# Gate and up gradients of a SwiGLU backward pass: four half-token stores per group from SyncE in place of sixteen from ScalarE, silu and its slope in quarters

## The chip, the cores and the metric

The kernel runs on one core of one Trainium2 chip. The metric is the device time of one execution in microseconds (us), as the median of several. A core has a matrix engine (TensorE, PE in the profile; its weight loads are PEld), a vector engine (VectorE, DVE), an activation engine (ScalarE, ACT), a general engine (GpSimd, POOL) and SyncE (SP), which here does nothing but issue transfers. Each engine works off its own instructions strictly in the order in which the compiler laid them down. An instruction that has to wait holds up everything behind it on that engine. This holds for the instruction that starts a transfer too: it sits in the queue of the engine that issues it.

## The reference

The forward function is `x + s * g`. `xn` is the layer norm of `x` (2048 tokens by 576), `s` is a state-space convolution of `xn`, and `g` is silu of a SwiGLU feed-forward network with 4608 hidden units. The kernel returns the output and the gradients of `x` and of all parameters. For the part that the change touches, only this matters:

```python
gate = xn @ w1                       # 2048 x 4608
up   = xn @ w3
h    = silu(gate) * up
out  = h @ w2
# backward, with go the gradient of out (2048 x 576):
gh    = go @ w2.T                    # 2048 x 4608
gup   = gh * silu(gate)              # "gu" in the kernel
ggate = gh * up * silu'(gate)        # "gg" in the kernel
gw2 = h.T @ go;  gw3 = xn.T @ gup;  gw1 = xn.T @ ggate
gxn = ggate @ w1.T + gup @ w3.T + (gradient through the convolution)
```

## The kernel before

The program has a forward half and a backward half. In the forward half, `gate` and `up` are computed and kept in device memory (`G_dram`, `U_dram`), in the layout [group, 128 partitions, 16 token tiles, 256 hidden units]. The backward half is laid out by `backward` (line 1062) and has three strands that share the engines:

- the convolution's backward (`conv_bwd_quarter`, four quarters), then the gradients of its parameters (`param_quarter`, 36 chunks; each loads a transposed `qT` on SyncE and works mainly on VectorE, lines 971 and 974);
- the **groups** of the feed-forward network, 18 of 256 hidden units each. A group is an elementwise half (`phase6_elementwise`) and a half that forms weight gradients (`phase6_weight_grads`), which is laid down one group later;
- `phase6_inputs`, which needs the gate and up gradients of all groups, and so comes last. For each of the 16 token tiles it reads them back, transposed by the transfer itself (`ggc`, `guc`, issued on SyncE), and multiplies them with the transposed weights.

The order on each engine comes from a planner. Calls of `self.at(us)` give each piece a due time, which serves as its priority; the planner simulates the engines and picks, whenever one is free, the ready instruction with the earliest priority. Groups are due every 36 us from 700, quarters of the convolution every 60 us from 700, chunks of the parameters every 16 us from 940, so that the strands interleave.

The elementwise half of one group goes like this. GpSimd loads two raw blocks of `w2` (`w2r6`, line 1131), fills them up (1132), and SyncE transposes them into `w2T` (1133, which runs the helper on line 1115). GpSimd loads `gate` into `gg_n` (1137) and `up` into `h_n` (1138), 1 MB each. ScalarE forms silu into `gu_n` (1139) and silu's derivative over `gg_n` (1140), one instruction each over all 16 token tiles, 4096 elements in each partition. VectorE multiplies with `up` in four slices (1143, 1144). Then come four steps (loop at 1146), each over four token tiles: two of the first half of the tokens and two of the second. In a step, TensorE forms `gh` in two PSUM tiles `ph` (1157, 20 matmuls, three `ph` buffers in all), ScalarE copies both to `gh6` (1160), and VectorE multiplies `gh6` into `gu_n` and `gg_n` (1163). After each of these two products ScalarE issues two stores (1166) of two token tiles each. A group has sixteen stores of 128 KB.

The weight half accumulates over all 16 token tiles into `pgw` tiles in PSUM, of which there are two. Two rounds of two tiles give the `w2` gradient (1183, copied by ScalarE on 1187 into `gw2`), eight rounds give those of `w3` and `w1` (1194, copied on 1197 into `gw13`), and one gives the 64 remaining rows of both (1201 and 1203, copied on 1206). GpSimd issues the store of each copy (1188, 1198, 1207, 1208). The pool of `gw2` and `gw13` has two buffers of each, the pool of `gh6` two.

Of the kernel before, what the change touches and what calls it, by code (L numbers as in the profile page):

```python
# [10 lines left out]
ACT = mybir.ActivationFunctionType  # L11
# [49 lines left out]
class K:  # L61
# [1000 lines left out]
    def backward(self, T0, TG, TQ, TC, TX, gctx, mats):  # L1062
        nc, cfg = self.nc, self.cfg
        D, L, LT, F, FT = cfg.D, cfg.L, cfg.LT, cfg.F, cfg.FT
        self.GG_dram = self.dram.tile([LT, P, F], BF16, name="GG_dram")
        self.GU_dram = self.dram.tile([LT, P, F], BF16, name="GU_dram")
        self.GXN_dram = self.dram.tile([P, LT, D], FP32, name="GXN_dram")
        NG = F // self.FG
        T2 = T0 + TG * NG
        FA = 12  # L1070
        pool = self.tc.tile_pool
        PS = bass.MemoryType.PSUM
        with ExitStack() as out:
            ffn = ExitStack()
            wp = ffn.enter_context(pool(name="e_w", bufs=2))
            inp = ffn.enter_context(pool(name="e_in", bufs=2))
            elp = ffn.enter_context(pool(name="e_el", bufs=2))
            gwp = ffn.enter_context(pool(name="e_gw", bufs=2))
            ps_h = ffn.enter_context(pool(name="e_ps_h", bufs=3, space=PS))
            ps_gw = ffn.enter_context(pool(name="e_ps_gw", bufs=2, space=PS))  # L1080
            ps = out.enter_context(pool(name="b_ps", bufs=3, space=PS, side="right"))
            self.ssm_bwd_conv(T0, TQ, ps)
            mats.close()
            fix = out.enter_context(pool(name="b_fix", bufs=1, side="right"))
            S_all = fix.tile([P, 4, D], FP32, name="S_all")
            wA = out.enter_context(pool(name="x_wA", bufs=1, side="right"))
            self.at(T2 - 150)
            wT = [self.load_wT(wA, 0, FA)]
            T1 = T0 + 4 * TQ
            self.ssm_bwd_params(T1, TC, S_all, ps)  # L1090
            self.at(T1 + TC * D // 16)
            self.phase5_final(out, fix, S_all, ps)
            for gi in range(NG + 1):
                self.at(T0 + TG * gi)
                if gi < NG:
                    tiles = self.phase6_elementwise(gi, wp, inp, elp, ps_h)
                if gi > 0:
                    self.phase6_weight_grads(gi - 1, prev, self.go_o, gwp, ps_gw)
                prev = tiles
            ffn.close()  # L1100
            gctx.close()
            self.phase6_inputs(T2, TX, FA, wT)
# [14 lines left out]
    def phase6_elementwise(self, gi, wp, inp, elp, ps_h):  # L1117
        nc, cfg = self.nc, self.cfg
        D, DT, LT = cfg.D, cfg.DT, cfg.LT
        aps = self.aps  # L1120
        FG = self.FG
        nfl = FG // P
        nfull = D // P
        rem = D - nfull * P
        LH = LT // 2
        assert 2 * rem == P
        w2T = wp.tile([P, nfl, DT, P], BF16, name="w2T")
        for fl in range(nfl):
            fi = gi * nfl + fl
            w2r = wp.tile([P, DT * P], BF16, name="w2r6")  # L1130
            nc.gpsimd.dma_start(out=w2r[:, 0:D], in_=aps["B_w2"][fi * P:(fi + 1) * P, :])
            nc.gpsimd.tensor_copy(out=w2r[:, D:DT * P], in_=w2r[:, nfull * P:D])
            self.nat_transpose(w2T[:, fl], w2r[:])
        gg = inp.tile([P, LT, FG], BF16, name="gg_n")
        hn = inp.tile([P, LT, FG], BF16, name="h_n")
        gu = inp.tile([P, LT, FG], BF16, name="gu_n")
        nc.gpsimd.dma_start(out=gg[:], in_=self.G_dram[gi])
        nc.gpsimd.dma_start(out=hn[:], in_=self.U_dram[gi])
        nc.scalar.activation(out=gu[:], in_=gg[:], func=ACT.Silu)  # L1139
        nc.scalar.activation(out=gg[:], in_=gg[:], func=ACT.Derivative_silu)  # L1140
        for s in range(4):
            sl = slice(s * LT // 4, (s + 1) * LT // 4)
            nc.vector.tensor_tensor(out=gg[:, sl, :], in0=gg[:, sl, :], in1=hn[:, sl, :], op=ALU.mult)
            nc.vector.tensor_tensor(out=hn[:, sl, :], in0=gu[:, sl, :], in1=hn[:, sl, :], op=ALU.mult)
        pair = lambda t_: t_[:].rearrange("p (j t) f -> p j t f", j=2)
        for s in range(LH // 2):
            gh = elp.tile([P, 2, 2, FG], BF16, name="gh6")
            ph = [ps_h.tile([P, 2, FG], FP32, name="ph") for _ in range(2)]
            for k in range(2):
                t = s * 2 + k  # L1150
                for j in range(2):
                    tt = j * LH + t
                    rs = slice(j * rem, (j + 1) * rem)
                    steps = [(self.goT[:, c, tt * P:(tt + 1) * P], w2T[:, :, c, :]) for c in range(nfull)]
                    steps.insert(nfull * (1 - j), (self.goTt[rs, t * P:(t + 1) * P], w2T[rs, :, nfull, :]))
                    for n, (lw, rh) in enumerate(steps):
                        nc.tensor.matmul(ph[j][:, k, :].rearrange("p (a f) -> p a f", f=P), lhsT=lw, rhs=rh, start=(n == 0),  # L1157
                                         stop=(n == nfull))
            for j in range(2):
                nc.scalar.copy(out=gh[:, j], in_=ph[j][:])  # L1160
            sl = slice(s * 2, s * 2 + 2)
            for (dst, t_) in ((self.GU_dram, gu), (self.GG_dram, gg)):
                nc.vector.tensor_tensor(out=pair(t_)[:, :, sl], in0=gh[:], in1=pair(t_)[:, :, sl], op=ALU.mult)
                for j in range(2):
                    ts = slice(j * LH + s * 2, j * LH + s * 2 + 2)
                    nc.scalar.dma_start(out=dst[ts, :, gi * FG:(gi + 1) * FG].rearrange("t p f -> p t f"), in_=t_[:, ts, :])
        return hn, gg, gu

    def phase6_weight_grads(self, gi, tiles, go_o, gwp, ps_gw):
# [196 lines left out]
```

## Time and profile before

| | |
|---|---|
| time, median of 3 | 2269.04 us (2255.82 to 2273.89) |
| profiled execution | 2250.77 us, span of the core 2249.0 us |
| mean granted TensorE clock | 0.93 |
| busy: PE, DVE, ACT, POOL | 82%, 66%, 42%, 20% of the span |
| groups: first `ph` matmul to last `pgw` matmul | 875.7 to 1860.1 us |
| parameter chunks on VectorE (line 971) | 1325.7 to 2095.3 us |
| matmuls of `phase6_inputs` (line 1238) | 1872.9 to 2242 us |
| stores of line 1166 | 288 of 128 KB, issue 0.48 us, landing 3.4 us (medians) |

The profile lists, for each engine, how long it was busy, and for each idle stretch the instruction whose end released it ("releaser"). An instruction that starts a transfer isn't counted as busy time of its engine but occupies its queue all the same: time in which ScalarE is held by its own stores shows up as idle time of the copy behind them, with the transfer as its releaser. "issue" is time in which an engine waited for nothing that the profile shows.

### The profile page before, as it was taken

How to read it: one execution, taken by the hardware profiler on the slowest of the kernel's cores; microseconds unless marked ns; L12 is line 12 of the kernel's file. 1: busy time of each engine (PE TensorE's matmuls, PEld its weight loads, DVE VectorE, ACT ScalarE, POOL GpSimd, SP SyncE). 2: the span in 40 equal slices, each digit the busy share in tenths (PEclk: the TensorE clock that was granted, in tenths of full speed). 3: DMA queues.
4: the chain of work that ended last, by engine and by line, in shares of the span. 5: the costliest groups of instructions: out<-in, count | busy, mean ns of one | idle time of the engine just before them, and what ended most of it. 6: DMA issues, size and time to landing. Idle time of an engine off the chain costs nothing.

```text
span 2249.0 us, 41101 instructions
## 1 busy us (share of the span) xinstructions
PE 1842.5 (82%) x16141; PEld 1268.9 (56%) x16214; DVE 1488.6 (66%) x2842; ACT 950.1 (42%) x1608; POOL 459.0 (20%) x710
## 2 busy tenths in 40 slices
PE   2878888889996997887888857888888883899958
PEld 1533333345544675665767645666666672677736
DVE  7457888879872554887694976756666762186742
ACT  2958888875541114656464613334333330000000
POOL 4024555551122111201121111211111110000000
PEclk9989999999997998999999978999999996999979
DMA  3777777776569886454554579677777759999783
GB/s 76 269 253 261 267 265 264 261 245 240 195 157 244 190 203 160 139 146 118 154 156 143 155 184 198 182 186 150 177 191 176 177 126 199 183 218 221 152 126 77
DMA packets 620339, 420.76 MB, mean 187 GB/s; under 512 B 419504, under 2 KB 559920, under 8 KB 615536
## 3 DMA queue, kind: packets, MB, share of 16 engines
q1 hardware_dynamic: 482464, 240.40, 44.9%
q0 software_dynamic: 29520, 109.15, 15.2%
q10 hardware_dynamic: 108160, 68.57, 11.6%
q8 instruction: 127, 2.08, 0.4%
q14 instruction: 68, 0.56, 0.1%
HBM read 135.37 MB, written 190.37 MB: 145 GB/s over the span
## 4 chain that ended last, share of the span: by engine, by line
PE 26%; DVE 16%; DMA 14%; issue 9%; ACT 7%; SPq 4%; POOL 1%; ACTq 1%; POOLq 0%; DVEq 0%
PE px L1238 9%; SPq L1115 4%; PE pgw L1194 4%; PE ph L1157 3%; DMA w2T<-w2r 2%; PE et_ps L598 2%; DVE cm_t L622 2%; DMA qT<-Q_dram 2%; DMA out_dram<-gw 2%; PE pgw L1183 2%; DMA guc<-GU_dram 2%; ACT gg_n L1140 1%; ACT gu_n L1139 1%; PE pg L739 1%; PE pgw L1201 1%
## 5 line engine op out<-in xcount | busy, mean ns | idle before, releaser
L971 DVE TENSOR_TENSOR pr_q<-et_ps,pz 128x512 f32<-128x512 f32 x288 | 186.5, 684 | 171.6 <-PE et_ps L964 157.9
L1194 PEld LDWEIGHTS <-xn_bf 128*128 128x128 bf16 x2304 | 232.2, 101 | 85.7 <-issue 50.9
L1238 PE MATMUL px<-wTB_w,ggc 128*128 128x288 bf16 x1152 | 245.8, 293 | 35.2 <-DMA ggc<-GG_dram 13.7
L1238 PE MATMUL px<-wTB_w,guc 128*128 128x288 bf16 x1152 | 245.2, 293 | 29.6 <-DMA guc<-GU_dram 18.6
L739 PEld LDWEIGHTS <-xnT 128*128 128x128 bf16 x1152 | 108.7, 100 | 190.9 <-issue 93.5
L739 PE MATMUL pg<-wmB_w,xnT 128*128 128x512 bf16 x531 | 156.4, 399 | 57.9 <-DVE g_t L745 47.1
L974 DVE TENSOR_REDUCE S_all<-pr_q 128x8 f32<-128x512 f32 x288 | 185.3, 680 | 0.2
L1157 PE MATMUL ph<-w2T,goT 128*128 128x256 bf16 x1152 | 171.1, 283 | 12.5 <-DMA w2T<-w2r 6.7
L1183 PE MATMUL pgw<-go_o,h_n 128*128 128x288 bf16 x1152 | 166.0, 301 | 16.4 <-ACT gw L1187 16.0
L1194 PE MATMUL pgw<-gg_n,xn_bf 128*128 128x256 bf16 x1152 | 140.5, 283 | 36.5 <-ACT gw L1197 36.4
L794 PE MATMUL po<-w2g,hc 128*128 128x288 bf16 x1152 | 148.8, 292 | 17.5 <-DMA a<-UH_dram 17.3
L739 PE MATMUL pu<-wmB_w,xnT 128*128 128x512 bf16 x554 | 157.3, 395 | 6.5 <-ACT u_t L748 5.2
L1238 PEld LDWEIGHTS <-guc 128*128 128x128 bf16 x1152 | 114.7, 100 | 71.2 <-DMA guc<-GU_dram 20.3
L1157 PEld LDWEIGHTS <-goT 128*128 128x128 bf16 x1152 | 100.7, 100 | 86.4 <-issue 52.8
L1238 PEld LDWEIGHTS <-ggc 128*128 128x128 bf16 x1152 | 114.9, 100 | 59.3 <-issue 14.2
L1194 PE MATMUL pgw<-gu_n,xn_bf 128*128 128x256 bf16 x1152 | 140.4, 280 | 9.2 <-ACT gw L1187 7.6
L1197 ACT CAST gw<-pgw 128x256 bf16<-128x256 f32 x144 | 52.7, 389 | 224.6 <-DMA out_dram<-gw 89.8
L1255 ACT ACTIVATE t<-gx 128x576 f32<-128x576 f32 x16 | 11.0, 685 | 320.6 <-DVE gx L1241 285.6
L1183 PEld LDWEIGHTS <-h_n 128*128 128x128 bf16 x1152 | 115.7, 103 | 53.0 <-issue 17.7
L794 PEld LDWEIGHTS <-hc 128*128 128x128 bf16 x1152 | 113.6, 100 | 49.4 <-issue 18.2
L1160 ACT CAST gh<-ph 128x512 bf16<-128x512 f32 x144 | 81.1, 601 | 138.0 <-PE ph L1157 34.1
L1241 DVE TENSOR_TENSOR gx<-px,gxs 128x288 f32<-128x288 f32 x32 | 13.4, 452 | 179.4 <-PE px L1238 179.4
(308 smaller groups left out, 3971.6 us busy)
## 6 DMA issues: line engine op xcount, KB each, us to landing
G_dram<-g_t POOLq DMA_DIRECT2D x72, 256.0 KB, 3.5
U_dram<-u_t POOLq DMA_DIRECT2D x72, 256.0 KB, 4.1
H_dram<-h_t SPq DMA_DIRECT2D x72, 256.0 KB, 3.8
Q_dram<-q_k SPq DMA_DIRECT2D x36, 512.0 KB, 3.2
gg_n<-G_dram POOLq DMA_DIRECT2D x18, 1024.0 KB, 5.8
h_n<-U_dram POOLq DMA_DIRECT2D x18, 1024.0 KB, 6.1
GU_dram<-gu_n ACTq DMA_DIRECT2D x144, 128.0 KB, 3.3
GG_dram<-gg_n ACTq DMA_DIRECT2D x144, 128.0 KB, 3.5
```

The costliest lines, as they stand in the source:

```text
L598: nc.tensor.matmul(pv, lhsT=mat[:, kt, sl], rhs=V[:, :, ri, kt, :], start=(i == 0), stop=(i == n - 1))
L739: nc.tensor.matmul(pt[:], lhsT=xnT[:, c, ts], rhs=wm[w][:, c, :], start=(c == 0), stop=False)
L794: nc.tensor.matmul(po_[:, pi_, 0:pw], lhsT=hc[:, fi, :], rhs=w2[fi][:, po:po + pw], start=(fi == 0), stop=(fi == FT - 1))
L971: nc.vector.tensor_tensor(out=pr[:], in0=T[h][:].rearrange("p r d k a -> p (r d) k a"), in1=pz[:, dg, h, s:s + 2].rearrange("p r d a -> p ...
L974: nc.vector.tensor_reduce(out=S_all[:, 2 * s:2 * s + 2, d0:d0 + 4].rearrange("p k d -> p d k"), in_=pr[:].rearrange("p (r d) k a -> p d k ...
L1115: self.nc.sync.dma_start_transpose(out=dst, in_=src)
L1157: nc.tensor.matmul(ph[j][:, k, :].rearrange("p (a f) -> p a f", f=P), lhsT=lw, rhs=rh, start=(n == 0), stop=(n == nfull))
L1160: nc.scalar.copy(out=gh[:, j], in_=ph[j][:])
L1183: nc.tensor.matmul(pgw[pi_][:, 0:pw], lhsT=hn[:, tt, fl * P:(fl + 1) * P], rhs=go_o[:, tt, po:po + pw], start=(tt == 0), stop=(tt == LT - 1))
L1194: nc.tensor.matmul(pw_[:, 0:FG], lhsT=self.xn_bf[:, tt, c * P:(c + 1) * P], rhs=nat[:, tt, :], start=(tt == 0), stop=(tt == LT - 1))
L1197: nc.scalar.copy(out=gw[:], in_=pw_[:, 0:FG])
L1238: nc.tensor.matmul(px[pi_][:, 0:pw], lhsT=act[:, fi, :], rhs=wT[part][ai][:, f, po:po + pw], start=(fi == 0 and ai == 0), stop=(fi == FT - ...
```

## The change

The change has four parts. The stores of `gu_n` and `gg_n` move out of the loop of steps: a group now has four, each of eight token tiles (one half of the tokens) of one tensor, 512 KB, and they are issued by SyncE. Silu runs as four instructions of four token tiles each, and so does its derivative, so that VectorE can begin on a quarter. The pool of `gh6` grows from two buffers to three. The pool of `gw2` and `gw13` grows from two buffers of each to four. The aim is to take the issue of stores out of ScalarE's queue and to loosen the ties between ScalarE, VectorE and the stores.

```diff
@@ backward
-            elp = ffn.enter_context(pool(name="e_el", bufs=2))
-            gwp = ffn.enter_context(pool(name="e_gw", bufs=2))
+            elp = ffn.enter_context(pool(name="e_el", bufs=3))
+            gwp = ffn.enter_context(pool(name="e_gw", bufs=4))
@@ phase6_elementwise
-        nc.scalar.activation(out=gu[:], in_=gg[:], func=ACT.Silu)
-        nc.scalar.activation(out=gg[:], in_=gg[:], func=ACT.Derivative_silu)
-        for s in range(4):
-            sl = slice(s * LT // 4, (s + 1) * LT // 4)
+        quarters = [slice(s * LT // 4, (s + 1) * LT // 4) for s in range(4)]
+        for sl in quarters:
+            nc.scalar.activation(out=gu[:, sl, :], in_=gg[:, sl, :], func=ACT.Silu)
+        for sl in quarters:
+            nc.scalar.activation(out=gg[:, sl, :], in_=gg[:, sl, :], func=ACT.Derivative_silu)
+        for sl in quarters:
             nc.vector.tensor_tensor(out=gg[:, sl, :], in0=gg[:, sl, :], in1=hn[:, sl, :], op=ALU.mult)
             nc.vector.tensor_tensor(out=hn[:, sl, :], in0=gu[:, sl, :], in1=hn[:, sl, :], op=ALU.mult)
...
-            for (dst, t_) in ((self.GU_dram, gu), (self.GG_dram, gg)):
+            for t_ in (gu, gg):
                 nc.vector.tensor_tensor(out=pair(t_)[:, :, sl], in0=gh[:], in1=pair(t_)[:, :, sl], op=ALU.mult)
-                for j in range(2):
-                    ts = slice(j * LH + s * 2, j * LH + s * 2 + 2)
-                    nc.scalar.dma_start(out=dst[ts, :, gi * FG:(gi + 1) * FG].rearrange("t p f -> p t f"), in_=t_[:, ts, :])
+        for (dst, t_) in ((self.GU_dram, gu), (self.GG_dram, gg)):
+            for j in range(2):
+                ts = slice(j * LH, (j + 1) * LH)
+                nc.sync.dma_start(out=dst[ts, :, gi * FG:(gi + 1) * FG].rearrange("t p f -> p t f"), in_=t_[:, ts, :])
```

## The prediction

> **What bounds the kernel now.** I read the page first, for the engines' shares, then the busy time by stretches, then who waited for whom in the stretch of the groups (850 to 1850 us), TensorE first and ScalarE second, then the timeline of ScalarE over one group. The engines and three stretches (the columns are length, then busy time of PE, PEld, DVE, ACT and POOL with the number of instructions, then granted clock, DMA share and GB/s):
>
> ```profile
> PE 1842.5 (82%) x16141; PEld 1268.9 (56%) x16214; DVE 1488.6 (66%) x2842; ACT 950.1 (42%) x1608; POOL 459.0 (20%) x710
> ...
> 1100.00:1200.00 100.00, 87.35 (x893) 69.91 (x893) 80.09 (x166) 62.17 (x144) 16.62 (x26) 0.98 0.50 145
> ...
> 1500.00:1600.00 100.00, 81.97 (x691) 61.21 (x689) 67.06 (x112) 36.85 (x50) 18.70 (x37) 0.92 0.73 174
> 1600.00:1700.00 100.00, 84.33 (x730) 64.83 (x729) 61.80 (x103) 38.27 (x54) 20.29 (x41) 0.95 0.71 169
> ```
>
> TensorE is the busiest engine everywhere, at 81% (773.8 of 950 us from 850 to 1800), and ScalarE is far from full. So the groups are bound by TensorE plus the gaps in it, about 176 us up to 1800. What ends the gaps:
>
> ```profile
> PE ph L1157 <- ACT gh L1160: 44.3, 27, 7.3
> PE pgw L1194 <- ACT gw L1197: 37.4, 21, 10.7
> PE et_ps L964 <- DMA qT<-Q_dram: 17.5, 4, 10.2
> PE pgw L1183 <- ACT gw L1187: 16.0, 7, 7.5
> ...
> PE pgw L1194 <- ACT gw L1187: 7.6, 14, 2.9
> ```
>
> The columns are microseconds in total, times, longest. The four lines with ACT make 105.3 us, and all are PSUM copies of the groups: TensorE has a full PSUM tile and ScalarE hasn't emptied it. Why does an engine that is 42% busy come late? Its own waits answer:
>
> ```profile
> ACT gw L1197 <- DMA out_dram<-gw: 84.9, 34, 5.5
> ...
> ACT gw L1197 <- DMA GG_dram<-gg_n: 32.7, 4, 14.2
> ACT gh L1160 <- DMA GU_dram<-gu_n: 32.7, 7, 6.4
> ACT gw L1197 <- DMA GU_dram<-gu_n: 31.0, 6, 7.1
> ...
> ACT gh L1160 <- DMA GG_dram<-gg_n: 12.9, 2, 7.4
> ```
>
> Two holders stand out: ScalarE is held by the issue of its own stores (32.7 + 32.7 + 31.0 + 12.9 = 109.3 us), and a copy can't start because both `gw13` buffers are still being stored (84.9 us). The timeline of ScalarE in one group shows the first:
>
> ```profile
> 1491.23 1.04 ACTq L1166 DMA_DIRECT2D GU_dram<-gu_n  x2
> 1492.37 1.45 ACTq L1166 DMA_DIRECT2D GG_dram<-gg_n  x2
> 1493.92 1.68 ACTq L1166 DMA_DIRECT2D GU_dram<-gu_n  x2
> 1495.69 1.53 ACTq L1166 DMA_DIRECT2D GG_dram<-gg_n  x2
> 1497.34 0.37 ACT L1197 CAST gw<-pgw 128x256 bf16<-128x256 f32 x1 [5.86 <-DMA GU_dram<-gu_n]
> ```
>
> From 1491.2 to 1497.2 ScalarE does nothing but start eight stores, while a finished `pgw` tile waits.
>
> [...] 288 issues by 0.48 us are 138 us of ScalarE's queue. [...]
>
> **The change part by part.**
>
> *Stores off ScalarE.* Per step ScalarE has two `gh` copies (2 x 0.586 us, the median of line 1160) and four issues (4 x 0.48), 3.1 us; TensorE needs 2.4 us for the step's 20 matmuls (in the timeline at 1609 us, 10 come every 1.2 us). ScalarE is slower by 0.7 us a step, 2.8 us a group, 50 us over 18 groups. The measured `ph` wait is 44.3 us, so this account fits. Without the issues the step costs ScalarE 1.2 us, and a copy no longer stands behind a store that waits for VectorE. I take all 44.3 us as removed. The third `gh6` buffer belongs to this: VectorE may then lag three steps of a group's four.
>
> *Four `gw` buffers.* A round of line 1194 takes 3.65 us on TensorE; copy, issue and landing take 0.37 + 0.54 + 2.2 = 3.1 us, so two buffers do until GpSimd is held. It is held, in its turn, for the `w2T` transposes (119.9 us over 25 waits on line 1131). Example: the transposes are issued at 1591.0 and GpSimd is through its second `w2r` load at 1598.7, 7.7 us, a little over the two rounds (7.3 us) that two buffers cover. Four cover 14.6 us. With the stores gone as well, I take the 37.4 + 1.1 us of lines 1194 and 1201 behind `gw` 1197 as removed. Sum so far: 82.8 us.
>
> *Silu in quarters.* Six more activations per group by the fixed cost: [...] 0.16 us from the copies in the trace (0.373 us for 256 elements, 0.586 for 512: 0.83 ns each, 0.16 left). That is 1.0 to 1.1 us a group. Table loads stay at two a group, as copies between them needed none before. The first product on VectorE waits for 1.28 + 4 x 1.03 + 1.28 + 1.03 = 7.7 us after the load instead of 9.8. Silu has the earlier priority over the `gw` copies of the group before, so I don't expect copies to slip in between the quarters. Then the `gw` 1187 waits (16.0 + 7.6 us) stay, and ten or so of these get 1 us longer: +10 us. The earlier start of VectorE I cost at nothing: line 1163 is behind the `gh` copies and other strands' work (29.8 us of waits on `gh`).
>
> *Stores on SyncE.* This is the new wait. The nearest row is `gK_dram<-gk_st` (line 922): 576 KB in runs of 512 bytes like these stores, 0.65 us to issue, 5.0 us to land (4.7 to 8.2), two at a time. Four stores are 2.6 us of SyncE's queue, hidden by its idleness. But they wait for the last product of line 1163, a few us after the last `ph` matmul, and behind them stand the `w2T` transposes for the group after next, then `qT` and `gz` of the parameter chunks. The 2 MB need 9 us (at 1.13 MB per 5.0 us) to 15 us (per 8.2 us). Lower bound: the planner puts `w2T` first, as it is ready once `ph` ends, and nothing is lost. Upper bound: transposes land 10 to 15 us late each group. Then GpSimd's hold grows from 7.7 to about 18 us, 3 us beyond what four buffers cover, and `qT` (two buffers, one chunk per 21 us: 26 chunks from 1310 to 1865) is late too: 6.5 us a group or 117 us in all, as an estimate. I take 1.2 us a group, 22 us, since only the `w2T` part bites when stores go first, and they go first in perhaps half of the groups.
>
> *Sum.* -82.8 + 10 + 22 = -51 us. A tenth of it I give to waits that come up next (`qT`, VectorE at 80% in the convolution): -45 us. The last 389 us of the span, from the end of the groups, have none of these stores but the transposes of `ggc`, `guc` and weights on SyncE; nothing changes there. 2269 - 45 = **2224 us**.
>
> **The rivals.**
>
> *All of it goes* (0.15): the quarters let copies through and SyncE costs nothing, so all 106 us of copy waits vanish: 2163 us. For it: ScalarE then has about half of its queue free. Against it: the priorities just named.
>
> *Other waits take the place* (0.17): VectorE is 80% busy in the convolution's stretch and waits 145 us for `et_ps` in the parameters, so that in-order TensorE may find the next gap at once; about 10 us remain, 2259 us. Against it: most copy waits are within the group strand itself, where TensorE has some 41 us of work per group (its lines' busy time by 18) in a 48 us cycle.
>
> *SyncE becomes the holder* (0.18): the upper bound above, 2269 - 83 + 117 = 2303 us, **slower**. For it: `qT` already ends 17.5 us of TensorE's waits, and SyncE blocks in order. Against it: `w2T` is prefetched by two groups, and one chunk has 21 us where VectorE needs 11.
>
> **How the numbers follow.** The forecast (0.50) is 2224 us. Faster by over 1% means under 2246: forecast and first rival, 0.65; within 1%: 0.17; slower: 0.18. The range is 2160, where all copy waits are gone, to 2290, inside the SyncE case, which leaves out about 0.1 above and somewhat less below.
>
> **What would show it.** Right: `ph` behind `gh` and `pgw` 1194 behind `gw` 1197 fall from 82 us to under 25; ScalarE's waits on `out_dram<-gw` fall from 84.9 us to under 30; the group cycle from 1400 to 1850 shrinks from 48 to about 45 us; the four stores issue in about 0.65 us each; `gw` 1187 waits stay near 24 us; the tail after the groups stays near 389 us. Wrong: waits of TensorE on `qT`, `w2T` or GpSimd's on `w2T` that grow by more than 40 us; a SyncE queue held by the stores' issue for several us; table loads above 36; a lower granted clock that eats the closed gaps; or a longer tail, if the parameter chunks fall behind the groups.

## The result and the profile after

The changed kernel takes 2172.6 us (median of 4, 2159.7 to 2178.6) against 2270.2 us before: a ratio of 0.9574 with a 95% interval of 0.9516 to 0.9632, so 98 us less where the prediction said 45 us. 1% of the time before is 22.7 us; the shares below are turned into microseconds with it. The profiled executions, from which the lines come, are 91 us apart (2250.77 and 2159.66 us).

First the engines' line of the changed kernel's page, which answers to the one of before:

```profile
PE 1820.9 (84%) x16214; PEld 1260.4 (58%) x16214; DVE 1487.1 (69%) x2842; ACT 960.5 (45%) x1716; POOL 464.8 (22%) x710
```

The work is the same and the span is shorter. Where the time went is read from three stretches of each kernel: from the first `ph` matmul to the first parameter product on VectorE (the convolution), from there to the last `pgw` matmul (the parameter chunks), and the tail. Busy time by stretches, the kernel before (start and end, length, busy PE, PEld, DVE, ACT, POOL, then granted clock, DMA share, GB/s):

```profile
876.00:1326.00 450.00, 368.56 (x3647) 290.03 (x3645) 338.42 (x706) 244.63 (x558) 77.57 (x127) 0.94 0.54 149
1326.00:1862.00 536.00, 446.97 (x3856) 341.92 (x3853) 357.54 (x592) 195.54 (x277) 99.32 (x192) 0.93 0.74 174
1862.00:2249.00 387.00, 309.57 (x2476) 239.51 (x2472) 186.67 (x518) 15.62 (x38) 1.07 (x2) 0.90 0.92 170
```

The same for the changed kernel:

```profile
875.00:1314.00 439.00, 370.92 (x3712) 296.68 (x3709) 341.03 (x708) 253.70 (x613) 83.81 (x134) 0.94 0.55 155
1314.00:1782.00 468.00, 421.13 (x3788) 328.82 (x3787) 348.59 (x582) 199.29 (x330) 98.89 (x185) 0.94 0.77 198
1782.00:2158.00 376.00, 305.82 (x2478) 238.12 (x2475) 191.30 (x526) 15.58 (x38) 1.06 (x2) 0.91 0.90 175
```

The lengths say it: 450 to 439, 536 to 468, 387 to 376. Of 90 us, 68 were won where groups and parameter chunks run together. In the first two stretches, 79 us shorter, TensorE's busy time falls by 23.5 us (368.6 + 447.0 to 370.9 + 421.1) and its idle time by 55.5. Why the busy time falls, and what the tail's 11 us are, wasn't looked into.

Who waited for whom, changed kernel, TensorE, 850 to 1900 us (total us, times, longest; line numbers have moved by a few: 1159 is `ph`, 1162 the `gh` copy, 1197 and 1200 a round of `pgw` and its copy, 1186 and 1190 those of the `w2` gradient):

```profile
PE ph L1159 <- ACT gh L1162: 42.0, 16, 6.4
...
PE pgw L1197 <- ACT gw L1200: 8.8, 7, 3.5
...
PE ph L1159 <- DMA w2T<-w2r: 6.5, 1, 6.5
PE et_ps L964 <- DMA qT<-Q_dram: 6.5, 3, 3.3
...
PE pgw L1197 <- ACT gw L1190: 2.0, 3, 1.3
...
PE pgw L1186 <- ACT gw L1190: 1.2, 2, 0.9
```

The waits for `gw` copies fell from 61.0 us (37.4 + 16.0 + 7.6) to 12.0; the figures of before are read to 1850 us, to 1900 us the first is 38.0. Those for `gh` copies hardly fell: 44.3 to 42.0 us, in fewer and longer pieces. With the small ones, all copy waits fell from 107 to 55 us: 52 us, where the time of the two profiled executions fell by 91. SyncE's transposes, which were to suffer, hold TensorE less than before in these two traces: `qT` 17.5 to 6.5 us, `w2T` 6.7 to 6.5. ScalarE in the same stretch:

```profile
ACT gw L1200 <- DMA out_dram<-gw: 24.0, 11, 4.3
...
ACT gh L1162 <- DVE gg_n L1165: 18.1, 7, 5.8
```

The 109 us behind its own stores are gone, as they must be, and the wait for `gw` buffers fell from 84.9 us (89.8 when read to 1900 us) to 24.0. What holds the `gh` copies now is seen in the timeline of ScalarE, changed kernel:

```profile
1509.13 1.13 ACT L1162 CAST gh<-ph 128x512 bf16<-128x512 f32 x2 [2.31 <-PE ph L1159]
1510.28 1.28 ACT L1141 ACT_TABLE_LOAD   x1
1512.01 3.89 ACT L1141 ACTIVATE gu_n<-gg_n 128x1024 bf16<-128x1024 bf16 x4 [0.45 <-DMA gg_n<-G_dram]
1515.92 1.28 ACT L1143 ACT_TABLE_LOAD   x1
1517.21 2.00 ACT L1143 ACTIVATE gg_n<-gg_n 128x1024 bf16<-128x1024 bf16 x2
...
1521.02 1.53 ACT L1162 CAST gh<-ph 128x512 bf16<-128x512 f32 x3
```

Between two `gh` copies stands the whole block of silu and slope, 11 us with its table loads: with quarters, the planner laid no `gh` copy inside it from the third group on. TensorE meanwhile runs out of `ph` tiles; its timeline has the wait:

```profile
1521.63 0.27 PE L1159 MATMUL ph<-w2T,goTt 64*128 64x256 bf16 x1 [3.28 <-ACT gh L1162]
```

Laid over ScalarE's timeline, 11 of the 16 waits and 26.8 of the 42.0 us fall into this block. In the kernel before it was 8.7 us of 44.3, and ScalarE's own stores were being issued in 15.3 us of them, a third.

The stores on SyncE (line 1169; least, median and longest issue in ns, first and last start):

```profile
L1169 SPq DMA_DIRECT2D GU_dram<-gu_n x36: 382/524/2767, 898.2 to 1741.7; - x36
L1169 SPq DMA_DIRECT2D GG_dram<-gg_n x36: 371/1563/6108, 899.5 to 1744.5; - x36
```

The first two issue in 0.52 us, near the 0.65 us that was reckoned, the later two in 1.6 us and at worst 6.1 us. SyncE is held: from 1616.42 us two of these issues fill 8.05 us of its queue. What TensorE waits for its transposes is the 13.0 us above.

### The profile page after: what moved, and what is told of

Read it like the earlier page. It is cut to its first block, busy times and chain, and to the rows that moved or that the text cites. A ratio compares the mean times of both kernels' runs of the same rounds, so it can differ in the third digit from the quotient of the medians.

```text
span 2157.8 us, 40947 instructions
## 1 busy us (share of the span) xinstructions
PE 1820.9 (84%) x16214; PEld 1260.4 (58%) x16214; DVE 1487.1 (69%) x2842; ACT 960.5 (45%) x1716; POOL 464.8 (22%) x710
## 5 line engine op out<-in xcount | busy, mean ns | idle before, releaser
L1197 PEld LDWEIGHTS <-xn_bf 128*128 128x128 bf16 x2304 | 226.1, 98 | 41.6 <-issue 13.7
L739 PE MATMUL pg<-wmB_w,xnT 128*128 128x512 bf16 x576 | 162.5, 398 | 53.8 <-DVE g_t L745 42.2
L1159 PE MATMUL ph<-w2T,goT 128*128 128x256 bf16 x1152 | 186.7, 298 | 22.2 <-ACT gh L1162 15.6
L739 PE MATMUL pu<-wmB_w,xnT 128*128 128x512 bf16 x576 | 161.7, 396 | 5.2 <-ACT u_t L748 5.1
L1186 PE MATMUL pgw<-go_o,h_n 128*128 128x288 bf16 x1152 | 158.3, 291 | 4.1 <-DVE h_n L1146 2.9
L1159 PEld LDWEIGHTS <-goT 128*128 128x128 bf16 x1152 | 105.9, 105 | 89.3 <-issue 52.0
L1197 PE MATMUL pgw<-gg_n,xn_bf 128*128 128x256 bf16 x1152 | 130.1, 273 | 8.6 <-ACT gw L1200 8.6
L1197 PE MATMUL pgw<-gu_n,xn_bf 128*128 128x256 bf16 x1152 | 134.8, 276 | 2.5 <-ACT gw L1190 2.0
L743 ACT ACTIVATE s_t<-pg 128x512 bf16<-128x512 f32 x144 | 86.7, 602 | 99.3 <-PE pu L741 89.4
```

What stands on the lines that cost most here:

```text
L739: nc.tensor.matmul(pt[:], lhsT=xnT[:, c, ts], rhs=wm[w][:, c, :], start=(c == 0), stop=False)
L743: nc.scalar.activation(out=s_t[:, :, q, :], in_=pgv, func=ACT.Silu)
L1186: nc.tensor.matmul(pgw[pi_][:, 0:pw], lhsT=hn[:, tt, fl * P:(fl + 1) * P], rhs=go_o[:, tt, po:po + pw], start=(tt == 0), stop=(tt == LT - 1))
L1197: nc.tensor.matmul(pw_[:, 0:FG], lhsT=self.xn_bf[:, tt, c * P:(c + 1) * P], rhs=nat[:, tt, :], start=(tt == 0), stop=(tt == LT - 1))
```

## The experiments

The theories when the runs began: **A**, the parts add as in the prediction; **B**, the holders of ScalarE stand one behind another, so that taking one away shows the next; **C**, the planner lays down another order on every engine after any edit, and the order is the gain. In the traces, two kernels that differ in `gw` buffers alone have the same instructions in the same order on every engine; all other parts change the order, so only those pairs measure a wait alone.

All results, as ratios to the kernel before, which ran beside each of them (so medians of different rows don't compare exactly, ratios do):

| run | what it is | median us | ratio | 95% interval |
|---|---|---|---|---|
| changed kernel | all four parts | 2172.6 | 0.9574 | 0.9516 to 0.9632 |
| s_only | stores alone | 2228.7 | 0.9850 | 0.9809 to 0.9891 |
| q_only | quarters alone | 2297.8 | 1.0152 | 1.0098 to 1.0205 |
| g_only | four `gw` buffers alone | 2242.4 | 0.9917 | 0.9893 to 0.9941 |
| e_only | third `gh6` buffer alone | 2243.2 | 0.9907 | 0.9871 to 0.9943 |
| no_s | all but the stores | 2240.3 | 0.9899 | 0.9866 to 0.9931 |
| no_q | all but the quarters | 2163.2 | 0.9558 | 0.9514 to 0.9603 |
| no_g | all but the `gw` buffers | 2235.7 | 0.9875 | 0.9828 to 0.9922 |
| no_e | all but the `gh6` buffer | 2215.9 | 0.9799 | 0.9765 to 0.9832 |
| sg | stores and `gw` buffers | 2184.8 | 0.9675 | 0.9633 to 0.9716 |
| s4act | changed, four stores from ScalarE | 2218.1 | 0.9777 | 0.9738 to 0.9817 |
| s16sp | changed, sixteen stores from SyncE | 2199.7 | 0.9700 | 0.9663 to 0.9736 |
| p_before | before, groups due 1 us later | 2261.5 | 0.9978 | 0.9941 to 1.0015 |
| m6_before, p6_before | before, due 6 us earlier, later | 2247.3, 2246.5 | 0.9930, 0.9942 | 0.9905 to 0.9954, 0.9918 to 0.9966 |
| m6_after, p6_after | changed, due 6 us earlier, later | 2176.6, 2181.0 | 0.9611, 0.9657 | 0.9559 to 0.9663, 0.9590 to 0.9724 |
| best_g6 | no quarters, six `gw` buffers | 2138.2 | 0.9436 | 0.9374 to 0.9497 |
| best_g6e4 | the same, four `gh6` buffers | 2142.7 | 0.9492 | 0.9429 to 0.9555 |

### Each part alone

The stores alone, on the kernel before (the same lines as in the change):

```diff
-            for (dst, t_) in ((self.GU_dram, gu), (self.GG_dram, gg)):
+            for t_ in (gu, gg):
...
+        for (dst, t_) in ((self.GU_dram, gu), (self.GG_dram, gg)):
+            for j in range(2):
+                ts = slice(j * LH, (j + 1) * LH)
+                nc.sync.dma_start(out=dst[ts, :, gi * FG:(gi + 1) * FG].rearrange("t p f -> p t f"), in_=t_[:, ts, :])
```

> Only the stores: four of 512 KB per group from SyncE at the end of the group; two gh6 and two gw buffers, silu whole. Theory A (the stores held ScalarE, and what held it was long issues and the waits for VectorE's products): this part alone gives most of the gain, -50 to -70 us, about 2205 us, and ScalarE's 109 us of waits behind stores go to zero. Theory B (no part does it alone, since the holders of ScalarE stand one behind another: with the stores gone the gw copies still wait for GpSimd's stores): -15 to -30 us, and ACT gw <- DMA out_dram<-gw stays at 80 us or more. Theory C (the planner's new order of the instructions, which any edit of the groups brings, gives the gain): as much as any other part alone that changes the order.

Measured: -34 us (1.5%), between A and B, a little beyond B. What ScalarE waits for, stores alone:

```profile
ACT gw L1198 <- DMA out_dram<-gw: 147.8, 54, 7.0
```

It was 84.9 us before. The first holder went and the second grew by 63 us: that is B's picture, with a part of the gain getting through. TensorE's wait for `gh` copies didn't fall either: 54.6 us.

Silu and slope in quarters alone:

```diff
-        nc.scalar.activation(out=gu[:], in_=gg[:], func=ACT.Silu)
-        nc.scalar.activation(out=gg[:], in_=gg[:], func=ACT.Derivative_silu)
+        for sl in quarters:
+            nc.scalar.activation(out=gu[:, sl, :], in_=gg[:, sl, :], func=ACT.Silu)
+        for sl in quarters:
+            nc.scalar.activation(out=gg[:, sl, :], in_=gg[:, sl, :], func=ACT.Derivative_silu)
```

> Only silu and its slope in quarters. Theory A: no gain, 0 to +10 us, as six more activations per group cost ScalarE 1 us. Theory B: 0 within 10 us. Theory C: the order on all engines changes as much as with the stores, so a gain of 30 us or more would come from the order and not from a wait that was removed.

Measured: 35 us slower, which no theory had. The stretch of the parameter chunks grew from 536 to 575 us. TensorE's waits for copies grew from 107 to 138 us, and ScalarE's `gh` copies were held up by VectorE's parameter products (lines 971 and 974) for 66.6 us in place of 20.5. Whether the quarters do this or the order that came with them isn't separated.

Four `gw` buffers alone:

```diff
-            gwp = ffn.enter_context(pool(name="e_gw", bufs=2))
+            gwp = ffn.enter_context(pool(name="e_gw", bufs=4))
```

> Only four buffers of gw2 and gw13 in place of two. The order of the instructions is then the same as before on every engine, so this is the wait alone. Theory A: PE pgw <- ACT gw 1197 (38 us) falls by half or more, -20 to -35 us, as the prediction reckoned. Theory B: ScalarE is still held by its own stores behind it, -5 to -15 us, and the wait on out_dram<-gw falls far more than the time does. Theory C: 0 to -10 us.

Measured: -19 us (0.8%), between A and B; TensorE's wait on `gw` 1197 fell from 38.0 to 28.7 us, not by half. ScalarE's waits with this part alone:

```profile
ACT gh L1160 <- DMA GU_dram<-gu_n: 42.5, 8, 6.6
ACT gw L1197 <- DMA GG_dram<-gg_n: 34.1, 4, 15.5
ACT gw L1197 <- DMA GU_dram<-gu_n: 31.6, 6, 7.1
...
ACT gw L1197 <- DMA out_dram<-gw: 4.5, 3, 1.6
```

The wait on `out_dram` fell by 80 us, from 84.9 to 4.5, and the time by 19. What is in front now are ScalarE's own stores.

A third `gh6` buffer alone:

```diff
-            elp = ffn.enter_context(pool(name="e_el", bufs=2))
+            elp = ffn.enter_context(pool(name="e_el", bufs=3))
```

> The kernel before with three gh6 buffers in place of two. The prediction gave the third buffer nothing of its own; in the changed kernel it was worth 43 us. If holders stand one behind another, it shows little while the stores stand on ScalarE between the copies: within 10 us of before. If it is worth as much here (20 us or more faster), the parts add and the third buffer was simply overlooked.

Measured: -21 us (0.9%). The expectation of little was wrong. How much of it is the buffer and how much the order can't be told from this run; the order runs below give the scale.

### The order without a change of work

```diff
-                self.at(T0 + TG * gi)
+                self.at(T0 + TG * gi + 1)
```

> The kernel before with the groups' due times 1 us later in the planner, nothing else: some of the instructions change places. Theories A and B: within 10 us of before. Theory C: moves by 20 us or more either way are possible, and show how much a new order alone is worth.

Measured: no difference. Later the same edit with -6 and +6 in place of +1, on both kernels:

> The kernel before with the groups' due times 6 us earlier: nothing of the work changes, but about half as many instructions change places as with the stores or the quarters, and as many as with the third gh6 buffer. If the order is worth 20 us by itself (theory C), this one and its mirror image (6 us later) spread by 20 us or more around before, and then gains of 20 us of single parts that change the order can't be put down to a wait. If not, both are within 12 us.

> The kernel before with the groups' due times 6 us later. Theory C: 20 us or more from before, either way. Otherwise within 12 us.

> The changed kernel with the groups' due times 6 us earlier. If the changed kernel's gain beyond the sum of its parts were a lucky order, this and its mirror image lose it: 2195 us or more. If it is the waits, both stay within 15 us of 2173.

> The changed kernel with the groups' due times 6 us later. A lucky order: 2195 us or more. The waits: within 15 us of 2173.

On the kernel before both shifts are faster, by 0.7% and 0.6% (16 and 13 us); on the changed kernel both medians are higher, by 0.4% and 0.8%, within overlapping intervals. Neither reaches the 20 us of theory C, both are beyond the 12 us of the others. So an order by itself was worth up to some 16 us in these tries, and a few orders don't set a limit: single gains of 20 us that come with a new order aren't proof of a wait. The 98 us aren't a lucky order: shifted, the changed kernel keeps 0.9611 and 0.9657.

### Each part taken from the changed kernel

The edits are the ones above, reversed.

> The changed kernel with the sixteen stores of a group back on ScalarE, in the loop of steps; quarters, three gh6 and four gw buffers stay. Singly, the stores gave -34 us, the quarters +35, the gw buffers -20, which add up to -19 where the whole change gives -98. Theory B (one holder behind another): without the store part nearly all of the gain goes, 2250 us or more, as the quarters cost and the gw buffers can't show. Theory A (the parts add): 2173 + 34, about 2207 us.

Measured: 0.9899. Without the stores 3.25% or 74 us are lost: most of the gain, nearer to B, though B had 2250 us or more against 2240.

> The changed kernel with silu and its slope whole again. Theory A (the parts add; quarters alone were slower by 35 us): faster than the changed kernel, about 2140 us. Theory B: once the stores are off ScalarE the quarters help, since VectorE's products start sooner and the copies follow: 2190 us or more.

Measured: 0.9558 against 0.9574, no difference that can be told. Neither A (30 us faster) nor B (slower) holds. But the waits change places. TensorE without the quarters:

```profile
PE pgw L1195 <- ACT gw L1198: 27.2, 11, 9.4
PE ph L1157 <- ACT gh L1160: 24.5, 16, 3.3
```

With silu whole, the planner lays a `gh` copy between silu and its slope in 14 of the 18 groups, and the wait on `gh` is 24.5 us in place of 42.0; the waits on `gw` copies are about as much longer. All copy waits are 55 us in both. The pair differs in order too, so this is seen in the traces and not shown as the quarters' own doing.

> The changed kernel with two gw buffers again; the order of the instructions is exactly that of the changed kernel, so this is the wait alone. Theory A (the parts add): +20 us, 2193 us. Theory B: with ScalarE free, the out_dram stores are what holds the copies, so the buffers are worth more here than the 20 us they gave alone: +30 to +50 us, 2203 to 2223 us, with ACT gw <- DMA out_dram<-gw at 90 us or more.

Measured: 0.9875. In the same order, two buffers in place of four cost 3.0% or 68 us, where four in place of two gave 19 us alone. That is more than B's 30 to 50 us. ScalarE's wait without the `gw` buffers, and TensorE's behind it:

```profile
ACT gw L1200 <- DMA out_dram<-gw: 161.2, 52, 12.9
```

```profile
PE pgw L1197 <- ACT gw L1200: 48.2, 20, 10.3
```

The first was 24.0 us and the second 8.8 us with four. This is the clearest run of all.

> The changed kernel with two gh6 buffers again. Theory A: 0 to +10 us. Theory B: the third buffer lets ScalarE run ahead of VectorE's products, +10 to +25 us, with more wait of ScalarE's gh copies on VectorE's line 1165.

Measured: 0.9799. Without the third buffer 2.25% or 51 us are lost, more than either theory had and more than the shifted orders gave; but this order is another one too. ScalarE waits for VectorE's products 24.7 us in 16 pieces in place of 18.1 in 7; TensorE's wait on `gh` is 54.8 us in place of 42.0 and that on `qT` 29.0 in place of 6.5.

### Issuer or size of the stores

```diff
-                nc.sync.dma_start(out=dst[ts, :, gi * FG:(gi + 1) * FG]...
+                nc.scalar.dma_start(out=dst[ts, :, gi * FG:(gi + 1) * FG]...
```

> The changed kernel, but its four stores of 512 KB per group are issued by ScalarE, after the group's last product, in place of SyncE. If the engine is what counts (ScalarE stands behind every store that waits for VectorE[...]): 2215 to 2240 us, as with the sixteen stores on ScalarE (2240). If the number and place of the stores is what counts (four at the end of the group instead of sixteen within the steps): within 15 us of the changed kernel, 2160 to 2188 us.

The other way round, the sixteen stores within the steps as in the kernel before, with `nc.sync` for `nc.scalar`:

> The changed kernel, but with the sixteen stores of 128 KB in the loop of steps, issued by SyncE. If the engine is what counts: within 15 us of the changed kernel. If small stores within the steps hold SyncE's queue, as the prediction feared of the four: transposes of w2T and qT come late and TensorE waits for them by 20 us or more, 2195 us or more.

With the changed kernel and the run without the stores' part these make a square, all else as in the changed kernel but for the order, which differs in all four:

| | sixteen in the steps | four at the end |
|---|---|---|
| from ScalarE | 0.9899 | 0.9777 |
| from SyncE | 0.9700 | 0.9574 |

From ScalarE to SyncE is worth 2.0% in both columns (45 and 46 us), from sixteen to four 1.2 to 1.3% in both rows (28 and 29 us). The expectations had taken one or the other; both seem to count, though a difference of 28 us isn't far above what an order gave. With sixteen stores on SyncE TensorE waits 27.7 us for transposes (`qT` 20.4, `w2T` 7.3) in place of 13.0: 15 us more, where the expectation had 20 or more.

### Which parts need each other, and the best version

Stores and `gw` buffers together, without quarters and with two `gh6` buffers, in exactly the order of the stores alone:

> Stores on SyncE and four gw buffers, silu whole, two gh6 buffers. The order is exactly that of the run with the stores alone (2229 us), so against it this is the gw buffers alone once ScalarE doesn't issue the stores. If the buffers' worth comes from the stores' leaving (one holder behind another): 50 to 65 us, 2165 to 2180 us, and the third gh6 buffer adds little to it (2163 without quarters). If the buffers are worth the same 20 us as on the kernel before: 2209 us, and the third gh6 buffer makes up the rest.

Measured: 0.9675. The `gw` buffers give 1.75% (40 us) once the stores are off ScalarE, against 0.83% (19 us) on the kernel before, each in one order. That is one holder behind another, at somewhat less than the 50 us expected. Stores and `gw` buffers make 74 us together; the third `gh6` buffer adds 1.2% or 27 us (0.9675 to 0.9558), in another order, where the expectation had little. TensorE's wait for `gh` copies with these two parts, to be set against 44.3 us before and 24.5 with the third buffer:

```profile
PE ph L1157 <- ACT gh L1160: 52.8, 21, 9.8
```

The run without quarters with six `gw` buffers, in its order, and then with four `gh6` buffers:

```diff
-            elp = ffn.enter_context(pool(name="e_el", bufs=3))
-            gwp = ffn.enter_context(pool(name="e_gw", bufs=4))
+            elp = ffn.enter_context(pool(name="e_el", bufs=4))
+            gwp = ffn.enter_context(pool(name="e_gw", bufs=6))
```

> The changed kernel with silu whole and six gw buffers; the order of instructions is that of the run without quarters (2163 us), so against it this is the buffers alone. There TensorE still waits 23 us for gw copies in the parameter chunks' stretch, and ScalarE 44 us for out_dram. If that is what is left to get: 2140 to 2152 us, and the wait on out_dram under 10 us. If four buffers are already enough: 2160 us or so.

> Silu whole, stores on SyncE, six gw buffers and four gh6 buffers, one for each step of a group, so that no gh copy waits for VectorE's products of the same group. If gh copies behind those products are still what TensorE waits for: 10 us or more under 2138 us. If three are enough: within 10 us of 2138.

Six `gw` buffers give another 1.2% (28 us): 2138 us beats both kernels, by 5.6% and by 1.4%. The wait on `out_dram` fell from 44.1 to 22.5 us only, not under 10. The fourth `gh6` buffer gives nothing more (0.9492 with an interval that overlaps 0.9436).

## Why the prediction was right and wrong

**The direction was right, and the mechanism in part.** TensorE's gaps were the bound and ScalarE's copies ended most of them. For the `gw` copies the account holds: the same buffers, in one order each, gave 19 us with the stores on ScalarE, 40 with them on SyncE and 68 as the last part. For the `gh` copies it doesn't.

**What failed.** The prediction was 53 us short. The steps, in its own terms and in the order of their size:

- "I take all 44.3 us as removed. The third `gh6` buffer belongs to this." With the stores gone and two `gh6` buffers, TensorE waited 52.8 us for `gh` copies, not nothing. The third buffer, priced at nothing of its own, was worth 27 us without quarters and 51 us with them, of which a new order may be up to 16 or so.
- "I take 1.2 us a group, 22 us" for SyncE, against 82.8 us for the stores and the `gw` buffers: 60.8 us net. Together (sg) they gave 74 us, SyncE's cost included. How the 13 us divide is open. TensorE's waits on `qT` and `w2T` fell from 24.2 to 13.0 us in place of growing, but this hangs on the order: with due times shifted by 6 us they are 7.3 and 13.4 us on the kernel before, 24.7 and 33.7 on the changed one. So a cost of SyncE isn't excluded.
- "Then the `gw` 1187 waits [...] stay, and ten or so of these get 1 us longer: +10 us". The 1 us fits: a quarter took 1.04 us in the changed kernel (median of lines 1141 and 1143), silu or slope as a whole 3.62 in the kernel before (lines 1139 and 1140), with a table load of 1.28 us ahead of each of the two in both kernels; eight quarters are 1.1 us more a group than two whole ones. But the waits fell from 23.6 to 3.2 us, and the quarters measured 0.9574 against 0.9558, nothing that can be told. The tenth for waits to come (5 us) can't be seen either.

One after another the measured steps are 74 us for stores and `gw` buffers, 27 for the third buffer and -4, within the noise, for the quarters: 97 us, where the prediction had 61, 0, and -15. They make up the whole by construction, as each starts where the last one ends, and the last two come with a new order each.

**Right for a wrong reason.** The reckoning of a step (3.1 us of ScalarE against 2.4 of TensorE, 50 us in all) fitted the 44.3 us by chance: ScalarE was issuing its stores in only 15.3 us of them. Once the stores had gone, the block of silu and slope stood in the way, in 26.8 of the 42.0 us. Likewise the `gw` buffers' 38.5 us were neither their worth alone (19) nor last (68). A table of waits names the last holder, not what is gained by removing it: the copy waits fell by 52 us between two executions that are 91 us apart.

**Other points.** ScalarE's wait on `out_dram` under 30 us: right (24.0). Table loads at two a group: right, 18 and 18. The tail, where nothing was to change: 387 to 376 us by the same stretch. The four stores at 0.65 us each: right for two, the others 1.6 us and up to 6.1, which had been named as a sign of being wrong. The group cycle at about 45 us: 42 (47 before, from silu to silu over the last seven or eight groups). `ph` and `pgw` waits together under 25 us: wrong, 50.8 (42.0 + 8.8). The rival "all of it goes" gave 2163 us for the right amount by a path that didn't happen, as the copy waits went to 55 us and not to nothing. The rivals of other waits and of SyncE as the new holder are out, as both had little or no gain.

**Open.** Why the quarters alone cost 35 us while they cost nothing in the changed kernel: order and work change together there, and 35 us is more than the shifts of the order gave. For the stores, too, and for the third `gh6` buffer no pair in one order exists, so wait and order aren't separated below some 16 us.

## What to carry to other kernels

Where an engine that empties PSUM also issues stores, try taking the stores off it and giving the tiles it fills more buffers in one go: here each was worth 19 to 34 us alone and 68 to 74 us as the last one missing. Price a wait by what stands next behind it in that engine's queue, not by its own line in the table. When a scheduler lays a new order after every edit, shift due times without changing any work to learn what an order alone is worth, before believing gains of that size.

## What the hardware showed that was not expected

A wait of TensorE of 2.06 us was followed by 3.41 us at half the granted clock, and so cost more than its length. Kernel before, busy time in four pieces of one group, before, during and after a wait of 2.06 us for a `gw` copy at 1495.7 us:

```profile
1490.00:1493.40 3.40, 3.40 (x32) 2.93 (x32) 2.94 (x6) 1.36 (x4) 1.07 (x2) 1.00 1.14 319
1495.70:1497.80 2.10, 0.04 (x3) 0.07 (x2) 2.10 (x5) 0.46 (x2) 0.92 (x2) 1.00 1.13 291
1498.50:1501.90 3.40, 3.40 (x18) 2.44 (x17) 3.40 (x7) 0.00 (x0) 1.56 (x4) 0.50 0.73 214
1502.00:1505.40 3.40, 2.61 (x25) 2.18 (x24) 0.93 (x2) 0.65 (x2) 1.07 (x2) 1.00 0.06 20
```

In the third piece the granted clock is 0.50, and 18 matmuls run in 3.4 us where 32 ran before. The 32 matmuls of line 1194 behind the wait took 5.32 us, those at 1490.75 us 3.66: 1.66 us more, on top of the 2.06. Not every such wait cost this: behind one of 2.00 us that ended at 1547.79 us the clock stayed at 1.00, and the 32 took 3.65 us.

In the trace of the kernel before the record of the clock has 88 entries, each at 1.00 or 0.50, and all but the last have a length that is a whole multiple of 3.413 us. Cut into steps of that length, it has 549 at 1.00 up to the last matmul. In 40 of them TensorE was busy for less than 45% of the step, and a step at 0.50 followed each time; in 499 it was busy for at least 50%, and none followed; of the 10 between, 3 were followed by one. The step of this wait, from 1495.10 us, has 40%. Of 91 steps at 0.50, 45 were at least 80% busy, and a step at 1.00 followed 43 of them; it followed none of the other 46. In the changed kernel the counts are less clear-cut: 31 of 36 steps below 45% and 4 of 486 at 50% or more were followed by one at 0.50, and 36 of 39 at least 80% busy and 2 of 42 others by one at 1.00. These are counts of two executions; what decides the clock isn't shown by them.

The stretch of the parameter chunks with two `gw` buffers (the changed kernel without that part), and with six and silu whole:

```profile
1325.00:1849.00 524.00, 437.65 (x3792) 336.05 (x3790) 349.06 (x582) 198.58 (x329) 97.07 (x185) 0.91 0.70 177
```

```profile
1308.00:1746.00 438.00, 405.44 (x3742) 321.43 (x3740) 348.93 (x582) 191.74 (x265) 105.06 (x181) 0.98 0.85 211
```

The slower has 95 us at half the clock, with TensorE busy in 77 of them, the faster 20 and 14. If half of that busy time is lost (18 matmuls ran where 32 did, above), the loss is 39 and 7 us: as an estimate, at most 32 of the 86 us between them, which differ in quarters and order too. Over the groups of the kernel before and of the changed one the same estimate gives 48 and 44 us, so the clock isn't the main cause of the miss.
